# Four small moves in the order of an attention and feed-forward kernel on one core

## The chip, the core and the metric

The kernel runs on one core of a Trainium2 chip. A core has five engines that work side by side, each through its own queue of instructions, in order: TensorE (PE, matrix products and transposes; its weight loads are listed as PEld), VectorE (DVE), ScalarE (ACT), GpSimd (POOL) and SyncE (SP, which here only issues transfers). PE writes its results to PSUM, eight banks of 128 x 512 fp32 words; the others read PSUM or SBUF. Engines wait for each other through semaphores. The metric is the time of one execution in microseconds. The three runs of the kernel before took 175.51, 175.60 and 176.47 us; the median is 175.6.

## The reference

Windowed attention with a few global keys, and then a feed-forward part with the largest of three products. Batch 4, 8 heads, 768 positions, head dimension 64; 8 global keys, a window of 96; model width 512, inner width 768.

```python
scores = scale * np.matmul(q, k.transpose(0, 1, 3, 2))
is_global = pos[None, :] < n_global
is_local = (rel >= 0) & (rel < n_local)          # rel = row position - column position
dist = np.where(is_global & ~is_local, n_local, np.abs(rel))
scores = np.where(is_global | is_local, scores - slopes * dist, -1e9)
a = softmax(scores)                              # 1e-9 added to the sum
x = (a @ v), heads joined                        # 3072 x 512
h = np.maximum(np.maximum(x @ w1, x @ w2), x @ w3)
out = h @ w_out                                  # 3072 x 512, float32
```

## The kernel before

The 3072 rows are 24 tiles T of 128 rows, six to a batch. Two tiles (256 positions) form a group G, in which q and k are loaded, cast to bf16 and transposed together. Because the window is 96, tile T needs only its own keys, those of tile T - 1, and the 8 global keys, which are copied into rows of tile T - 1 that the window can't reach. The feed-forward part works on chunks of 4, 2, 2, 4, 4, 4 and 4 tiles (`SIZES`).

Nothing schedules this program. Its order is a string, `SCHEDULE`, of 782 units, written out in the source; the loop at the end of the kernel calls one small function for each. The place of a unit in the string sets its place in the queue of its engine and nothing else: units of different engines drift apart as far as the semaphores let them. A unit reads as a letter, its arguments, often with the engine last (0 ACT, 1 DVE, 2 POOL, 3 a DMA), and after `@` the buffer or bank that it takes. Those that the text needs:

- `l a.G.p` (SP, lines 229 and 236): load q (a = 0), k (1) or v (2) of group G, 512 KB in 512-byte pieces. `l0.7.2` is q of group 7, tiles 14 and 15.
- `c a.G.p.how` (lines 195 and 201): cast q or k of the group to bf16. On ACT or DVE it is one instruction of 128x1024, on POOL two of 128x512. `v T.e.how` (254) casts half of a tile's v.
- `X T` (SP, 292): transpose a tile's q and k by a DMA, from SBUF to SBUF. `G` (313, 315) and `V` (321 to 325) copy global keys and values.
- `S T.g` (PE, 349): scores of four heads; `e` (ACT, 356): their exponentials; `m` (DVE, 365 and 367): times the bias and window mask; `A T` (PE, 391 and 394): times v; `n T` (DVE, 402 and 403): divide by the sum, into `xb`.
- `Z T` (SP, 424): transpose the attention output of a tile by a DMA, from `xb` to `xT`; for a few tiles `t` and `u` do that on PE and ACT (418, 421).
- `F c.f.j` (PE, 433): 128 inner columns f of product j for chunk c, four matmuls. `f` (447, 449, 452) empties the bank: j = 0 a cast, j = 1 a maximum, j = 2 a maximum into `ht`.
- `O c.t` (PE, 457): one output tile, six matmuls; `o` (471) copies it to SBUF; `s` (SP, 477) stores it, in one transfer, or in two halves where the last argument is 2. `E` (PE, 457; 462, 463): the four output tiles of the last chunk, copied and stored as they come, the last of them in pieces of 256, 128 and 128 columns, the first two stored by SP and the third by ACT's own queue.

A bank or buffer that a unit takes has to be free: `F3.1.2@4` and then `A13@4` take bank 4, so A13 waits until `f3.1.2.1` has read it. A wait of the first instruction in a queue holds everything behind it.

Around the changed places the string reads, before (units of all engines):

```
Z8@0 V10.1.0 l0.7.2@2 v11.1.2 ... n10 ... Z9 ... m12.1.1 e13.0@2 c0.7.2.1@1 Z10 f2.0.1.1 m13.1.1
v13.0.1 l1.9.2@0 c1.9.2.1 F3.0.2@0 F3.0.1@5 f3.0.1.1 F3.1.2@4 f3.0.2.1@1 ... l1.7.2@6 c1.7.2.2 f3.1.2.1
V16.1.2 f4.3.0.0@0 v20.0.2 G18.0 ... c0.11.2.2@1 ... V16.0.2 ... c0.10.2.2@2 A19@2 ... G19.0 s0.1 V19.0.2
f6.5.2.1 E@7 O5.0@2 o5.0.0@5 s5.0.2
```

Of the kernel before, what the change touches and what calls it, by code (L numbers as in the profile page):

```python
# [21 lines left out]


SCHEDULE = """
    l0.12.1@0 l1.12.1@1 D10.512@0 l1.12.3@2 l0.12.2@3 l0.12.3@4 R K7 K6 B1.1 K4 B2.1 K2 B3.0 K1 K5 B0.1 B6.1
# [28 lines left out]
    v15.1.2 v12.1.2 F2.5.2@0 O1.1@1 v12.0.2 S12.1.0@2 e12.1@3 S13.1.0@4 m11.0.1 Z9 f2.5.2.1 S13.0.0@6
    o1.1.1@5 F2.4.2@0 A11@2 n11@2 F2.0.1@1 e13.1@1 F2.3.1@4 m12.0.1 m12.1.1 e13.0@2 c0.7.2.1@1 Z10 f2.0.1.1
    m13.1.1 F2.0.2@5 f2.3.1.1 t11@2 F2.1.2@3 l0.9.2@3 l1.8.2@4 u11.0 G13.0 f2.1.2.1 f2.0.2.1 F2.3.2@6
    F3.4.0@2 F3.0.0@1 f3.4.0.0@4 f3.0.0.1@0 m13.0.1 v13.1.1 f2.4.2.1 F3.1.0@4 F3.3.0@5 c0.9.2.0@2 f3.3.0.0@1
    A12@2 n12@1 f2.3.2.1 f3.1.0.1@2 F3.1.1@1 f3.1.1.1 v13.0.1 l1.9.2@0 c1.9.2.1 F3.0.2@0 F3.0.1@5 f3.0.1.1
    F3.1.2@4 f3.0.2.1@1 F3.2.0@1 F3.2.2@2 l1.7.2@6 c1.7.2.2 f3.1.2.1 F3.5.0@3 A13@4 V13.1.1 f3.5.0.1@3 n13@0
    l2.9.2@2 l0.8.2@5 c0.8.2.2@0 v19.0.2 V13.0.0 f3.2.0.0@0 v14.0.2 F3.5.1@0 l2.8.2@1 F3.2.1@6 f3.2.1.1  # L60
    f3.2.2.1 F3.3.1@1 F3.5.2@3 v18.1.0 X14@3 v14.1.2 X15 f3.5.1.1 f3.3.1.1 F3.4.1@2 c1.8.2.0 S14.0.0@4
    S14.1.0@0 e14.0@6 G14.2 f3.4.1.1 F3.4.2@6 f3.5.2.1 F3.3.2@7 e14.1@7 f3.4.2.1 m14.0.1 m14.1.1 v19.1.2
    v15.0.2 S15.0.0@0 e15.0@0 S15.1.0@2 G15.1 e15.1@5 f3.3.2.1 O2.0@6 A14@0 V14.1.2 o2.0.1@6 n14@3 X18@0
    O2.1@7 v18.0.0 o2.1.0@7 m15.0.1 S18.0.0@0 S18.1.0@2 X19 Z13@1 V14.0.1 O3.3@6 m15.1.1 e18.0@3 e18.1@4
    X16@1 o3.3.0@8 A15@0 n15@2 O3.0@7 S19.1.0@0 v17.1.1 m18.0.1 S16.1.0@2 m18.1.1 e19.1@1 S16.0.0@4 O3.2@6
    o3.0.1@9 e16.0@2 V15.1.2 A18@0 e16.1@6 n18@0 o3.2.1@10 m16.1.1 X17 O3.1@7 G16.0 Z14 o3.1.0@11 m16.0.1
    V15.0.1 S17.0.0@0 v16.0.0 Z12 S19.0.0@2 Z15 e19.0@7 S17.1.0@4 e17.1@0 m17.1.1 F4.4.0@6 e17.0@5 l0.11.2@1
    s1.0 l2.10.2@0 F4.2.0@7 l1.10.2@2 F4.1.0@2 F4.5.0@3 v16.1.0 F4.3.0@0 A16@4 f4.2.0.0@2 Z18@2 V16.1.2
    f4.3.0.0@0 v20.0.2 G18.0 F4.1.2@1 f4.1.0.1@3 c0.11.2.2@1 m17.0.1 v17.0.1 l2.11.2@2 n16@3 s3.1 f4.5.0.0@4
    V16.0.2 m19.0.1 l0.10.2@3 F4.0.1@0 F4.1.1@7 m19.1.1 f4.4.0.0@1 F4.5.2@6 c0.10.2.2@2 A19@2 Z16 n19@1 Z19  # L70
    G19.0 s0.1 V19.0.2 s2.1 f4.1.1.1 f4.1.2.1@0 V19.1.1 F4.0.0@4 F4.4.1@5 A17@2 c1.10.2.0 f4.0.0.1@3 n17@2
    F4.5.1@7 f4.5.1.1 F4.2.1@1 F4.3.2@4 f4.5.2.1 f4.4.1.1 F4.0.2@2 F4.3.1@3 F4.4.2@5 f4.2.1.1 v22.1.1
    f4.0.1.1 f4.3.1.1 f4.0.2.1 f4.3.2.1 F4.2.2@1 Z17 F5.1.1@0 F5.2.0@3 F5.5.0@2 s1.1 F5.3.0@4 F5.0.0@6
    f4.2.2.1 f5.3.0.0@4 f5.0.0.0@3 v21.1.2 F5.1.0@1 s0.0 l1.11.2@0 F5.3.1@4 c1.11.2.2 f5.2.0.1@0 f4.4.2.1
    v23.0.2 F5.0.1@3 v21.0.2 f5.1.0.1@2 f5.1.1.1 s2.0 X20@2 S20.0.0@0 v22.0.1 S20.1.0@6 f5.0.1.1 G20.2
    f5.5.0.0@1 e20.0@3 e20.1@4 F5.5.1@2 f5.5.1.1 F5.2.2@3 v20.1.2 f5.3.1.1 F5.2.1@5 m20.1.1 F5.4.0@2
    f5.2.1.1 m20.0.1 f5.2.2.1@1 F5.1.2@4 f5.1.2.1 X21 f5.4.0.0@0 s3.3 X23@3 s0.3 S21.1.0@0 S21.0.0@6 e21.0@2
    F5.0.2@3 X22 f5.0.2.1 v23.1.2 e21.1@6 s0.2 A20@4 F5.4.1@2 V20.0.1 m21.0.1 F5.4.2@3 G21.1 S22.1.0@0
# [533 lines left out]
```

## Time and profile before

| | |
|---|---|
| median of three runs | 175.6 us |
| span of the profiled execution, first to last instruction | 174.8 us |
| mean granted clock of PE | 0.996 |
| PE busy | 165.9 us, 95% |
| DVE busy | 131.9 us, 75% |
| ACT busy | 95.4 us, 55% |
| POOL busy | 54.7 us, 31% |
| read from and written to HBM | 25.17 and 6.29 MB |

The page gives the profiled execution's span alone; the time of that execution as the runs measure it is not on the page, and the median of the runs lies 0.8 us above the span. "L433" is line 433 of the kernel. A row of a timeline gives the start in us, the busy time, the engine, the line, the operation, what it writes and reads, how many instructions were merged, and in brackets how long the engine had been idle and what ended that. Row ends can overlap the next start by some 0.08 us on DVE and ACT, and on PE by more, since its instructions are pipelined and their ends are modelled. A transfer has two times: SP's row is the time that issuing took, and the landing is listed separately, counted from the issue.

### The profile page before, as it was taken

Reading aid. Unit: us, or ns where it says so; the run is one execution under the profiler, and the core shown is the slowest. Engines: PE = TensorE matmul, PEld = TensorE weight load, DVE = VectorE, ACT = ScalarE, POOL = GpSimd, SP = SyncE. Lnnn points to the kernel's source line nnn. Section 1 sums busy time; section 2 is a strip of 40 time slices with the busy share of each in tenths; the row PEclk is TensorE's granted clock in tenths of the full one; section 3 lists DMA queues with packets and bytes.
Section 4 is the critical chain, followed back from the end, with each engine's and each line's share of the span. In section 5 each row is a group of like instructions: output and inputs, shape, how many; then the busy total and the mean of one; then the engine's idle time right before and its main releaser. Section 6 shows DMA issues by size and latency. Waiting matters only on the chain.

```text
span 174.8 us, 3865 instructions
## 1 busy us (share of the span) xinstructions
PE 165.9 (95%) x1485; PEld 93.6 (54%) x1507; DVE 131.9 (75%) x268; ACT 95.4 (55%) x147; POOL 54.7 (31%) x99
## 2 busy tenths in 40 slices
PE   7997999999999999898999999999999999999991
PEld 2555745577676877544445545544445554444460
DVE  7889864988599897989898678899578993074910
ACT  5988897672868788440667688200345651402051
...
GB/s 149 352 292 327 402 360 385 270 371 311 229 303 179 139 183 266 267 290 284 165 135 112 114 145 306 305 210 260 231 213 20 0 120 137 121 286 4 0 119 185
DMA packets 66403, 37.36 MB, mean 214 GB/s; under 512 B 24144, under 2 KB 61392, under 8 KB 66384
## 3 DMA queue, kind: packets, MB, share of 16 engines
...
q10 hardware_dynamic: 144, 0.07, 0.1%
q14 instruction: 7, 0.06, 0.1%
HBM read 25.17 MB, written 6.29 MB: 180 GB/s over the span
## 4 chain that ended last, share of the span: by engine, by line
PE 76%; DVE 10%; DMA 6%; ACT 3%; issue 2%; SPq 0%; DVEq 0%
PE psum L433 44%; PE psum L457 17%; PE psum L349 6%; DMA xT<-xb 3%; DMA rawqk<-in_k_dram 3%; DVE P L365 3%; PE psum L391 3%; PE psum L394 2%; PE psum L276 2%; DVE ht L452 1%; DVE xb L403 1%; ACT P L356 1%; PE psum L270 1%; DVE qb L195 1%; PE psum L335 1%
## 5 line engine op out<-in xcount | busy, mean ns | idle before, releaser
L433 PE MATMUL psum<-xT,w 128*128 128x512 bf16 (+1 forms) x491 | 97.5, 348 | 1.5 <-DMA xT<-xb 0.7
L433 PEld LDWEIGHTS <-w 128*128 128x128 bf16 x504 | 47.6, 98 | 42.9 <-DMA xT<-xb 0.9
L356 ACT ACTIVATE P<-psum 128x1024 bf16<-128x1024 f32 (+1 forms) x48 | 43.3, 954 | 10.4 <-PE psum L349 10.3
L449 DVE TENSOR_TENSOR h<-h,psum 128x512 bf16<-128x512 bf16 (+1 forms) x42 | 25.0, 605 | 15.9 <-PE psum L433 12.4
L457 PE MATMUL psum<-wo,ht 128*128 128x512 bf16 (+2 forms) x147 | 33.4, 362 | 0.5
L447 ACT CAST h<-psum 128x512 bf16<-128x512 f32 (+1 forms) x27 | 13.8, 523 | 33.1 <-PE psum L433 29.8
L452 DVE TENSOR_TENSOR ht<-h,psum 128x512 bf16<-128x512 bf16 (+1 forms) x42 | 26.2, 644 | 2.1 <-PE psum L433 0.9
L365 DVE TENSOR_TENSOR P<-P,wmask 128x1024 bf16<-128x1024 bf16 x34 | 25.2, 752 | 2.0 <-ACT P L356 1.7
L457 PEld LDWEIGHTS <-ht 128*128 128x128 bf16 x156 | 13.8, 98 | 13.5 <-DVE ht L452 0.2
L254 POOL CAST va<-rawv 64x512 bf16<-64x512 f32 x28 | 18.5, 668 | 4.8 <-DMA rawv<-in_v_dram 3.7
L323 POOL COPY va<-vaf 4x260 int32<-4x260 int32 x17 | 7.2, 424 | 34.9 <-PE psum L394 34.5
L403 DVE TENSOR_TENSOR xb<-psum,rz 128x512 bf16<-128x512 f32 x24 | 16.6, 692 | 0.8
L201 POOL CAST qb<-rawk 128x512 bf16<-128x512 f32 x12 | 7.5, 654 | 23.7 <-DMA rawk<-in_k_dram 23.7
L349 PE MATMUL psum<-qkT 64*128 64x128 bf16 x352 | 14.4, 217 | 0.5 <-DVE qkT L315 0.4
L391 PEld LDWEIGHTS <-P 128*128 128x128 bf16 x192 | 12.6, 97 | 3.2 <-ACT P L356 0.4
L349 PEld LDWEIGHTS <-qkT 64*128 64x128 bf16 x352 | 10.0, 94 | 7.9 <-issue 5.9
L391 PE MATMUL psum<-va,P 128*128 128x65 bf16 x160 | 12.7, 193 | 0.7 <-DVE ht L452 0.6
L447 DVE CAST h<-psum 128x512 bf16<-128x512 f32 (+1 forms) x15 | 9.1, 615 | 5.1 <-PE psum L433 5.1
L471 ACT COPY staging<-psum 128x512 f32<-128x512 f32 x14 | 8.2, 592 | 8.8 <-PE psum L457 8.8
L201 POOL CAST qb<-rawq 128x512 bf16<-128x512 f32 x14 | 8.9, 664 | 9.0 <-DMA rawq<-in_q_dram 5.0
L394 PEld LDWEIGHTS <-P 128*128 128x128 bf16 x160 | 10.5, 97 | 2.1 <-issue 0.7
L394 PE MATMUL psum<-va,P 128*128 128x65 bf16 x128 | 9.9, 193 | 0.0
...
## 6 DMA issues: line engine op xcount, KB each, us to landing
...
out_dram<-staging SPq DMA_DIRECT2D x5, 128.0 KB, 2.2
```

Of the source, the lines that this page charges most:

```text
L254: copies[how](heads(va(T))[64 * e:64 * e + 64, :, 0:D], src)
L349: nc.tensor.matmul(sp[:, hh, j2, ds], qT(T - ds, 1, hsl, jp), qT(T, 0, hsl, jp), start=not how, stop=True, skip_group_check=True)
L356: nc.scalar.activation(P[:, :, 0:n], sps[T, g].rearrange("p a b d n -> p (a b) d n")[:, :, 0:n], AF.Exp, bias=0.0, scale=scale)
L365: mul(P, P, wmask[:, g, :, 0:2])
L391: nc.tensor.matmul(o, P[:, i, 0], heads(va(T))[:, h], start=True, stop=(t == 0), skip_group_check=True)
L394: nc.tensor.matmul(o, P[:, i, 1], heads(va(T - 1))[:, h], start=False, stop=True, skip_group_check=True)
L403: nc.vector.tensor_tensor(out=x.rearrange("p (g h) d -> p g h d", g=2), in0=o4[:, :, :, 0:64], in1=rz[:, :, :, None].to_broadcast([128, 2, ...
L433: nc.tensor.matmul(ps, w123[f // 2][:, j, dm, (f % 2) * 128:(f % 2) * 128 + 128], xT[c][:, dm], start=(dm == 0), stop=(dm == 3))
L447: copies[how](h01, ps)
L449: nc.vector.tensor_max(h01s[c, f], h01s[c, f], ps)
L452: nc.vector.tensor_max(dst, h01s[c, f].rearrange("p (t e i) -> p t e i", e=2, i=64), ps.rearrange("p (t e i) -> p t e i", e=2, i=64))
L457: nc.tensor.matmul(po, ht[c][:, f, tt * 128:(tt + 1) * 128], wo[:, f, cols], start=(f == 0), stop=(f == NF - 1))
```

## The change

All four moves are in the string; no function changes, and the numbers of all units but three stay as they are.

1. `l0.7.2`, the load of q for group 7, is issued after the transposes `Z9` and `Z10` instead of before them. Its cast `c0.7.2.1` on DVE moves from after `m12.1.1` to after `v13.1.1`.
2. The casts of k for groups 9 and 7 swap engines: `c1.9` goes from DVE to POOL, `c1.7` from POOL to DVE, there behind `f3.0.1.1`. The load `l1.7.2` is written earlier, with the same neighbours in SP's queue.
3. POOL's order around tile 19: before `V16.1, v20.0, c0.11, V16.0, c0.10, V19.0`; after `V16.1, V16.0, V19.0, v20.0, c0.11, c0.10`.
4. `O5.0`, its copy and its store come before `E` instead of after it, and the store is one transfer instead of two halves. The last piece of the program is then E's 128-column part.

In the diff most lines differ only because the string is wrapped anew; cut to the units that move:

```diff
-    ... Z8@0 V10.1.0 l0.7.2@2 v11.1.2 v15.1.2
+    ... Z8@0 V10.1.0 v11.1.2 v15.1.2
...
-    ... m12.0.1 m12.1.1 e13.0@2 c0.7.2.1@1 Z10 f2.0.1.1
+    ... m12.0.1 m12.1.1 e13.0@2 Z10 l0.7.2@2 f2.0.1.1
...
-    f3.4.0.0@4 f3.0.0.1@0 m13.0.1 v13.1.1 f2.4.2.1
+    f3.4.0.0@4 f3.0.0.1@0 m13.0.1 v13.1.1 c0.7.2.1@1 f2.4.2.1
...
-    ... v13.0.1 l1.9.2@0 c1.9.2.1 F3.0.2@0 F3.0.1@5 f3.0.1.1
-    F3.1.2@4 f3.0.2.1@1 F3.2.0@1 F3.2.2@2 l1.7.2@6 c1.7.2.2 f3.1.2.1
+    ... v13.0.1 l1.9.2@0 l1.7.2@6 c1.9.2.2 F3.0.2@0 F3.0.1@5 f3.0.1.1
+    c1.7.2.1 F3.1.2@4 f3.0.2.1@1 F3.2.0@1 F3.2.2@2 f3.1.2.1
...
-    ... V16.1.2 f4.3.0.0@0 v20.0.2 G18.0 F4.1.2@1 f4.1.0.1@3 c0.11.2.2@1 m17.0.1
-    ... s3.1 f4.5.0.0@4 V16.0.2 m19.0.1 ... F4.5.2@6 c0.10.2.2@2 A19@2 Z16 n19@1 Z19 G19.0 s0.1 V19.0.2 s2.1
+    ... V16.1.2 V16.0.2 f4.3.0.0@0 G18.0 F4.1.2@1 f4.1.0.1@3 m17.0.1
+    ... s3.1 f4.5.0.0@4 m19.0.1 ... F4.5.2@6 A19@2 V19.0.2 v20.0.2 c0.11.2.2@1 c0.10.2.2@2 Z16 n19@1 Z19 G19.0 s0.1 s2.1
...
-    F6.5.0@1 f6.5.0.1@2 F6.5.2@5 f6.5.1.1 f6.5.2.1 E@7 O5.0@2 o5.0.0@5 s5.0.2
+    F6.5.0@1 f6.5.0.1@2 F6.5.2@5 f6.5.1.1 f6.5.2.1 O5.0@2 o5.0.0@5 s5.0 E@7
```

More of the change, by code (lines that the diff above doesn't have):

```diff
@@ L54 @@
[L54 to L78, printed above, removed]
@@ L84 @@
-    f6.4.0.1@0 F6.1.1@4 f6.4.1.1 f6.4.2.1 s4.3 s4.0 f6.3.0.0@4 F6.3.2@1 F6.1.0@2 s5.2 F6.2.1@3 s4.2 s5.1
-    s4.1 f6.1.0.0@1 s3.0 s5.3.2 f6.3.1.1 f6.1.1.1 f6.3.2.1 f6.2.1.1 F6.2.2@2 f6.2.2.1 f6.1.2.1 F6.5.1@4
-    F6.5.0@1 f6.5.0.1@2 F6.5.2@5 f6.5.1.1 f6.5.2.1 E@7 O5.0@2 o5.0.0@5 s5.0.2
+    y1.0.1.1@1 y1.1.1.0 x12.0.2@0 e1.1@0 c1.12.2.1 x12.0.3 y0.0.0.1 l1.2.2@0 y1.0.0.1 x12.1.3@1 x12.1.2 y0.1.0.0
+    S0.1.1 e0.1@1 G0.1 b2.1@6 v2.0.2 v3.0.2 w1.0@0 S1.0.1 G1.0 e1.0@2 b2.0@2 w0.0@0 y1.1.0.1 S2.1.1 w1.1@1
@@ new lines @@
+    X12@2 G10.1 G12.1 F2.4.1@7 A9@4 V9.1.2 V9.0.2 X13 O1.0@6 l2.7.2@0 n9@0 S12.0.0@0 f2.4.1.1 m10.0.1 l2.6.2@1
+    v10.1.1 e12.0@4 S11.1.0@2 S11.0.0@4 e11.1@5 F2.2.2@7 f2.2.2.1@0 F2.3.0@0 F2.1.1@1 F2.0.0@7 f2.3.0.0@3
+    m10.1.1 e11.0@0 f2.0.0.0@1 A10@2 V10.0.2 f2.1.1.1 m11.1.1 o1.0.0@4 n10@3 Z8@0 V10.1.0 v11.1.2 v15.1.2
+    v12.1.2 F2.5.2@0 O1.1@1 v12.0.2 S12.1.0@2 e12.1@3 S13.1.0@4 m11.0.1 Z9 f2.5.2.1 S13.0.0@6 o1.1.1@5 F2.4.2@0
+    A11@2 n11@2 F2.0.1@1 e13.1@1 F2.3.1@4 m12.0.1 m12.1.1 e13.0@2 Z10 l0.7.2@2 f2.0.1.1 m13.1.1 F2.0.2@5
@@ new lines @@
+    f2.3.1.1 t11@2 F2.1.2@3 l0.9.2@3 l1.8.2@4 u11.0 G13.0 f2.1.2.1 f2.0.2.1 F2.3.2@6 F3.4.0@2 F3.0.0@1
+    f3.4.0.0@4 f3.0.0.1@0 m13.0.1 v13.1.1 c0.7.2.1@1 f2.4.2.1 F3.1.0@4 F3.3.0@5 c0.9.2.0@2 f3.3.0.0@1 A12@2
+    n12@1 f2.3.2.1 f3.1.0.1@2 F3.1.1@1 f3.1.1.1 v13.0.1 l1.9.2@0 l1.7.2@6 c1.9.2.2 F3.0.2@0 F3.0.1@5 f3.0.1.1
+    c1.7.2.1 F3.1.2@4 f3.0.2.1@1 F3.2.0@1 F3.2.2@2 f3.1.2.1 F3.5.0@3 A13@4 V13.1.1 f3.5.0.1@3 n13@0 l2.9.2@2
+    l0.8.2@5 c0.8.2.2@0 v19.0.2 V13.0.0 f3.2.0.0@0 v14.0.2 F3.5.1@0 l2.8.2@1 F3.2.1@6 f3.2.1.1 f3.2.2.1 F3.3.1@1
@@ new lines @@
+    F3.5.2@3 v18.1.0 X14@3 v14.1.2 X15 f3.5.1.1 f3.3.1.1 F3.4.1@2 c1.8.2.0 S14.0.0@4 S14.1.0@0 e14.0@6 G14.2
+    f3.4.1.1 F3.4.2@6 f3.5.2.1 F3.3.2@7 e14.1@7 f3.4.2.1 m14.0.1 m14.1.1 v19.1.2 v15.0.2 S15.0.0@0 e15.0@0
+    S15.1.0@2 G15.1 e15.1@5 f3.3.2.1 O2.0@6 A14@0 V14.1.2 o2.0.1@6 n14@3 X18@0 O2.1@7 v18.0.0 o2.1.0@7 m15.0.1
+    S18.0.0@0 S18.1.0@2 X19 Z13@1 V14.0.1 O3.3@6 m15.1.1 e18.0@3 e18.1@4 X16@1 o3.3.0@8 A15@0 n15@2 O3.0@7
+    S19.1.0@0 v17.1.1 m18.0.1 S16.1.0@2 m18.1.1 e19.1@1 S16.0.0@4 O3.2@6 o3.0.1@9 e16.0@2 V15.1.2 A18@0 e16.1@6
@@ new lines @@
+    n18@0 o3.2.1@10 m16.1.1 X17 O3.1@7 G16.0 Z14 o3.1.0@11 m16.0.1 V15.0.1 S17.0.0@0 v16.0.0 Z12 S19.0.0@2 Z15
+    e19.0@7 S17.1.0@4 e17.1@0 m17.1.1 F4.4.0@6 e17.0@5 l0.11.2@1 s1.0 l2.10.2@0 F4.2.0@7 l1.10.2@2 F4.1.0@2
+    F4.5.0@3 v16.1.0 F4.3.0@0 A16@4 f4.2.0.0@2 Z18@2 V16.1.2 V16.0.2 f4.3.0.0@0 G18.0 F4.1.2@1 f4.1.0.1@3
+    m17.0.1 v17.0.1 l2.11.2@2 n16@3 s3.1 f4.5.0.0@4 m19.0.1 l0.10.2@3 F4.0.1@0 F4.1.1@7 m19.1.1 f4.4.0.0@1
+    F4.5.2@6 A19@2 V19.0.2 v20.0.2 c0.11.2.2@1 c0.10.2.2@2 Z16 n19@1 Z19 G19.0 s0.1 s2.1 f4.1.1.1 f4.1.2.1@0
@@ new lines @@
+    V19.1.1 F4.0.0@4 F4.4.1@5 A17@2 c1.10.2.0 f4.0.0.1@3 n17@2 F4.5.1@7 f4.5.1.1 F4.2.1@1 F4.3.2@4 f4.5.2.1
+    f4.4.1.1 F4.0.2@2 F4.3.1@3 F4.4.2@5 f4.2.1.1 v22.1.1 f4.0.1.1 f4.3.1.1 f4.0.2.1 f4.3.2.1 F4.2.2@1 Z17
+    F5.1.1@0 F5.2.0@3 F5.5.0@2 s1.1 F5.3.0@4 F5.0.0@6 f4.2.2.1 f5.3.0.0@4 f5.0.0.0@3 v21.1.2 F5.1.0@1 s0.0
+    l1.11.2@0 F5.3.1@4 c1.11.2.2 f5.2.0.1@0 f4.4.2.1 v23.0.2 F5.0.1@3 v21.0.2 f5.1.0.1@2 f5.1.1.1 s2.0 X20@2
+    S20.0.0@0 v22.0.1 S20.1.0@6 f5.0.1.1 G20.2 f5.5.0.0@1 e20.0@3 e20.1@4 F5.5.1@2 f5.5.1.1 F5.2.2@3 v20.1.2
@@ new lines @@
+    f5.3.1.1 F5.2.1@5 m20.1.1 F5.4.0@2 f5.2.1.1 m20.0.1 f5.2.2.1@1 F5.1.2@4 f5.1.2.1 X21 f5.4.0.0@0 s3.3 X23@3
+    s0.3 S21.1.0@0 S21.0.0@6 e21.0@2 F5.0.2@3 X22 f5.0.2.1 v23.1.2 e21.1@6 s0.2 A20@4 F5.4.1@2 V20.0.1 m21.0.1
+    F5.4.2@3 G21.1 S22.1.0@0 S22.0.0@6 G22.0 e22.1@1 f5.4.1.1 e22.0@7 m21.1.1 f5.4.2.1 V20.1.1 n20@0 O4.0@2
+    m22.1.1 F5.3.2@3 f5.3.2.1 A21@0 n21@3 m22.0.1 S23.1.0@4 e23.1@0 S23.0.0@6 e23.0@5 O4.1@3 F5.5.2@0 m23.1.1
+    Z21@0 V21.1.1 m23.0.1 V21.0.2 A22@4 V22.0.2 V22.1.1 n22@1 s3.2 Z20 o4.1.0@4 O4.3@1 A23@6 O4.2@3 Z22
@@ new lines @@
+    o4.3.0@11 f5.5.2.1 O5.2@0 O5.3@1 n23@2 O5.1@4 o5.3.0@1 Z23 F6.4.2@1 o4.0.1@7 F6.0.0@2 F6.0.2@5 F6.0.1@6
+    o5.2.0@5 F6.1.2@0 o5.1.0@3 F6.4.0@4 F6.2.0@7 f6.0.0.0@2 f6.0.1.1 F6.4.1@2 f6.0.2.1@0 F6.3.1@5 o4.2.0@6
+    f6.2.0.1@3 F6.3.0@3 f6.4.0.1@0 F6.1.1@4 f6.4.1.1 f6.4.2.1 s4.3 s4.0 f6.3.0.0@4 F6.3.2@1 F6.1.0@2 s5.2
+    F6.2.1@3 s4.2 s5.1 s4.1 f6.1.0.0@1 s3.0 s5.3.2 f6.3.1.1 f6.1.1.1 f6.3.2.1 f6.2.1.1 F6.2.2@2 f6.2.2.1
+    f6.1.2.1 F6.5.1@4 F6.5.0@1 f6.5.0.1@2 F6.5.2@5 f6.5.1.1 f6.5.2.1 O5.0@2 o5.0.0@5 s5.0 E@7
```

54 lines of the change are left out of this document (22 added, 32 removed).

## The prediction

> **What bounds the kernel.** I read the page first, then a table of stretches, then the chain of waits, then the timelines of single engines around the places the change touches.
>
> ```profile
> span 174.8 us, 3865 instructions
> PE 165.9 (95%) x1485; PEld 93.6 (54%) x1507; DVE 131.9 (75%) x268; ACT 95.4 (55%) x147; POOL 54.7 (31%) x99
> L433 PE MATMUL psum<-xT,w 128*128 128x512 bf16 (+1 forms) x491 | 97.5, 348 | 1.5 <-DMA xT<-xb 0.7
> ```
>
> TensorE is busy 95% of the span, so no other engine's time counts by itself. A move can only pay where PE stands still, and the stretches say where that is (columns: stretch, length, then busy time of each engine, granted clock, DMA share, GB/s).
>
> ```profile
> 73.00:84.00 11.00, 10.36 (x68) 5.15 (x69) 9.23 (x18) 2.40 (x4) 2.15 (x3) 1.00 1.18 286
> 102.00:112.00 10.00, 9.78 (x84) 5.07 (x80) 7.68 (x13) 7.52 (x13) 2.92 (x5) 1.00 1.06 277
> 112.00:165.00 53.00, 52.68 (x361) 25.70 (x366) 38.57 (x69) 14.98 (x22) 6.68 (x13) 1.00 0.56 142
> 171.20:174.80 3.60, 0.00 (x0) 0.00 (x0) 0.00 (x0) 0.58 (x1) 0.00 (x0) 0.81 0.43 143
> ```
>
> From 112 to 165 us PE idles 0.32 us in 53, that is 0.06 per 10 us: this is what "full" looks like. Between 73 and 84 it idles 0.64, between 102 and 112 it idles 0.22, and after 171.2 nothing runs but one copy and its store. The timeline of PE shows the holes themselves.
>
> ```profile
> 71.12 1.04 PE L433 MATMUL psum<-xT,w 128*128 128x256 bf16 x8
> 72.81 3.63 PE L433 MATMUL psum<-xT,w 128*128 128x512 bf16 x15 [0.66 <-DMA xT<-xb]
> ...
> 83.12 0.19 PE L391 MATMUL psum<-va,P 128*128 128x65 bf16 x1 [0.59 <-DVE ht L452]
> ...
> 88.14 0.62 PE L349 MATMUL psum<-qkT 64*128 64x128 bf16 x16
> ```
>
> Two holes: 0.66 us at 72.81, where F3.4.0 waits for the transposed tile 10 (Z10), and 0.59 at 83.12, where A13 waits for f3.1.2.1 on DVE to empty its bank. The third figure to keep is 88.14, where S14 starts.
>
> **Move 1, l0.7 behind Z9 and Z10.** First SP's queue, with the landing times of three single transfers (us from issue: Z10's; a transpose with nothing ahead of it, issued at 139.99; X14's), and the line of an instruction fetch, which the view of transfers gives for 70.4 to 71.6 us and again for 86.9 to 88.3; then DVE; then ACT and POOL.
>
> ```profile
> 64.79 0.58 SPq L236 DMA_DIRECT2D rawq<-in_q_dram  x1
> 65.45 3.55 SPq L424 DMA_TRANSPOSE xT<-xb  x2
> 69.05 0.57 SPq L236 DMA_DIRECT2D rawq<-in_q_dram  x1
> 69.68 4.53 SPq L236 DMA_DIRECT2D rawk<-in_k_dram  x3
> ...
> 81.60 1.54 SPq L292 DMA_TRANSPOSE qkT<-qb  x1
> ```
> ```profile
> xT<-xb SPq DMA_TRANSPOSE x1, 5.0
> ...
> xT<-xb SPq DMA_TRANSPOSE x1, 2.4
> ...
> qkT<-qb SPq DMA_TRANSPOSE x1, 4.9
> ...
> q8 instruction: 1, 0.02, 5.6%
> ```
> ```profile
> 66.69 0.69 DVE L403 TENSOR_TENSOR xb<-psum,rz 128x512 bf16<-128x512 f32 x1
> ...
> 71.38 0.69 DVE L195 CAST qb<-rawq 128x1024 bf16<-128x1024 f32 x1
> ...
> 74.75 0.69 DVE L447 CAST h<-psum 128x512 bf16<-128x512 f32 x1 [0.74 <-PE psum L433]
> 75.36 0.68 DVE L365 TENSOR_TENSOR P<-P,wmask 128x1024 bf16<-128x1024 bf16 x1
> ...
> 79.51 0.43 DVE L254 CAST va<-rawv 64x512 bf16<-64x512 f32 x1
> 79.97 1.13 DVE L195 CAST qb<-rawk 128x1024 bf16<-128x1024 f32 x1
> ...
> 81.73 1.33 DVE L452 TENSOR_TENSOR ht<-h,psum 128x512 bf16<-128x512 bf16 x2
> ```
> ```profile
> 71.32 0.59 ACT L421 COPY xT<-psum 128x512 bf16<-128x512 bf16 x1 [0.57 <-PE psum L418]
> ...
> 79.94 1.63 POOL L201 CAST qb<-rawk 128x512 bf16<-128x512 f32 x2 [10.13 <-DMA rawk<-in_k_dram]
> ```
>
> Z9 now issues where l0.7 did, at 64.79. Z10 cannot issue before n10 ends (66.69 + 0.69 = 67.38), so it goes at about 67.45 instead of 67.78, with 512 KB less ahead of it. It lands between 67.45 + 2.4 = 69.9 and 67.45 + 5.0 = 72.45; I take about 70, since the load is gone. F3.4.0 then waits for nothing: the matmuls before it end at 71.12 + 1.04 = 72.16, and tile 11's copy on ACT at 71.32 + 0.59 = 71.91. So the hole of 0.66 at 72.81 goes.
>
> But what is late next is DVE. From 74.75 to 83.06 it runs almost without a pause, and A13 waits for its end. The chain starts at F3.0.0's eviction at 74.75, which now comes earlier: by 0.66, or by up to 0.8 if F3.4.0 can start at 72.0, since the 256-column matmuls before it are pipelined and their modelled ends lie late. Move 1 also carries c0.7 (0.69 us at 71.38) to behind v13.1.1, so from a place where DVE afterwards idled 0.74 into the chain itself. The chain's rest therefore starts between 0.03 later and 0.1 earlier; I take 0.1 earlier. Nearly all of the hole at 72.81 goes into that cast and comes back before A13.
>
> The price is on the loads. l0.7 used to run while Z9 and Z10 waited; now it is issued at about 67.45 + 1.2 = 68.7, near l0.9's old 69.05, and l0.9, l1.8, l1.9, l1.7, l2.9, l0.8 and l2.8 queue behind it. At 286 GB/s a 512 KB load takes 1.8 us. If the rings find other work all the while, the later loads lose nothing; if they stand empty for that whole time, 1.8. I take 0.7, nearer the lower end, because Z9, Z10 and the fetch fill part of it. POOL's wait shows l1.7 landing at 79.94, so it lands at about 80.6.
>
> **Move 2, c1.9 to POOL and c1.7 to DVE** (with l1.7's unit written earlier; its place in SP's order does not change). Before, the two casts ran at once: DVE's took 1.13 us, where the same 128x1024 cast alone took 0.69 (71.38). Now POOL takes c1.9 on its landing, some two microseconds ahead, and DVE does c1.7 after f3.0.1.1, with POOL idle: 1.13 - 0.69 = 0.44 off the chain. DVE reaches c1.7 at 79.51 - 0.1 + 0.43 + 0.7 = 80.54, about when l1.7 lands; I put that wait at 0.1. So f3.1.2.1 ends at 83.06 - 0.1 - 0.44 + 0.1 = 82.6 and A13 starts 0.45 earlier. Bounds: without the wait 0.55 gained; with l1.7 at 79.94 + 1.8 = 81.74 it ends at 81.74 + 0.69 + 1.33 = 83.76, 0.7 lost. POOL's queue behind c1.9 (c0.8, v19, v14) waits for l0.8 anyway. X14 needs c1.7: its end moves from 81.57 (POOL) to about 81.3.
>
> Where POOL's c1.9 meets v13.0.1 there may be a second price. See move 3's rows.
>
> **Move 3, POOL around tile 19.** DVE, POOL and SP there:
>
> ```profile
> 108.19 2.86 DVE L365 TENSOR_TENSOR P<-P,wmask 128x1024 bf16<-128x1024 bf16 x2
> ...
> 108.54 1.16 POOL L201 CAST qb<-rawq 128x512 bf16<-128x512 f32 x2
> ...
> 119.57 4.07 SPq L292 DMA_TRANSPOSE qkT<-qb  x2
> ```
>
> The two mask products of tile 19 took 2.86 us; one takes 0.68 (75.36), so the pair lost about 1.5 beside POOL's v20, c0.11 and V16.0. PE felt little of it: 0.22 - 0.06 = 0.16 idle between 102 and 112. Afterwards POOL does V16.0, then V19.0, which waits for A19, and only then the casts. m19 runs free, and PE gains between 0 and 0.16; I take 0.1. The casts now lie beside n19 and maxima that read PSUM. V16.0 comes earlier for A17; v20, c0.11 and c0.10 are first read by S20's side of the queue, whose transposes SP issues from 119.57 on, so a few microseconds of lateness cost nothing.
>
> The Trainium skill ("SBUF — State Buffer", section "Who interferes with whom") says that a DVE instruction with two SBUF inputs, or a copy or cast in a 2-port mode, is blocked for the whole length of a GpSimd instruction that holds the shared pair. This case's 2.86 us agree with it. By it, v13.0.1 would lose a half of POOL's c1.9 in move 2 if they meet; without it, nothing.
>
> **Move 4, E last.** O5.0 moves ahead of E; matmuls, copies and bytes are the same, so PE still ends at about 171.19.
>
> ```profile
> 167.67 3.15 SPq L463 DMA_DIRECT2D out_dram<-staging  x5
> ...
> 169.90 0.27 ACT L462 COPY staging<-psum 128x128 f32<-128x128 f32 x1 [0.30 <-PE psum L457]
> 170.19 0.37 ACTq L463 DMA_DIRECT2D out_dram<-staging  x1
> 171.19 0.58 ACT L471 COPY staging<-psum 128x512 f32<-128x512 f32 x1 [1.03 <-PE psum L457]
> 171.80 0.81 SPq L477 DMA_DIRECT2D out_dram<-staging  x2
> ```
> ```profile
> out_dram<-staging ACTq DMA_DIRECT2D x1, 64.0 KB, 2.1
> ...
> out_dram<-staging SPq DMA_DIRECT2D x2, 128.0 KB, 1.7
> ```
>
> Before, the end is a 0.58 copy and two issues: the second starts at about 172.2 and lands 1.7 to 1.8 later, at 174.0. Afterwards E's pieces come one O5.0 later (169.90 to 171.19 is 1.29): the last copy is 0.27, ACT issues at 170.19 + 1.29 = 171.48, SP's fifth store at about 170.41 + 1.29 = 171.7. With 2.1 to land, as those 64 KB stores took behind E's others, the end is at 173.8, 0.2 better. With the 1.7 of the stores that met no queue it is at 173.4, 0.6 better, and 0.8 if SP's five issues also run shorter than their 3.15. I take 0.4. O5.0 needs bank 2, which DVE empties before the last F6 matmuls; E's wait for ht 5 gets 1.29 us more cover.
>
> **Sum.** 0.45 + 0.1 + 0.4 = 0.95 us. The profiled span of 174.8 becomes 173.85. The median of the runs, 175.6, stands 0.8 above the span; the same gain on it gives 174.65, and I forecast 174.6.
>
> **Rivals.**
> (a) More is gained: l1.7 lands as before, A13 gains 0.55, A19 0.16, the tail 0.8: 1.5, so 174.1. For it: the tail before had two issues on one queue.
> (b) l1.7 lands 1.8 late, DVE holds its queue for it, and A13 loses up to 0.7: 0.7 - 0.1 - 0.4 = +0.2, 175.8. At 1.2 late it loses 0.1 and the sum is 175.2. For it: DMA share is 1.18 from 73 to 84, so nothing makes up for a gap. Against: the fetch and Z10's own packets overlap the gap.
> (c) POOL's c1.9 blocks v13.0.1 for one of its halves, 1.16 / 2 = 0.58: the 0.45 becomes -0.15, so 175.25. It needs l1.9 to land near 79, not 78.
> (d) Slower: X14 comes too late. It lands at 81.60 + 4.9 = 86.5, 1.64 before S14's 88.14. With the loads 1.8 late it lands at 88.3, and with an instruction fetch in its way (5.6% of 16 engines over 1.2 us is 1.1 us on one of them) at 89.4. PE then waits 1.26 at S14, less 0.1 and 0.3: 176.5. It decides from a landing after 88.14. Against: before, that later fetch came at 86.9, after X14 had landed, and X14 itself is issued no later than before.
> (e) Move 1 does not do what it says: Z10 was late through the fetch, not the load, and still lands near 72.8. Then c0.7 is 0.69 more in a chain that starts as before: 0.69 - 0.44 = +0.25 at A13, less 0.5: 175.35.
>
> **How the numbers follow.** A difference of 0.5% is 0.88 us, about what runs of this kernel can tell from none. Forecast 0.45 (own range 174.2 to 175.0; the bound lies at 174.72, so I put 0.28 of the 0.45 beyond it), (a) 0.2, (b) 0.1, (c) 0.08, (d) 0.1, (e) 0.07. Faster: 0.28 + 0.2 = 0.48; slower: (d) and 0.03 of (b) with more queueing, 0.13; same: the rest, 0.39. The range reaches from just under (a) to (b), 173.9 to 175.8, and leaves (d) and the tails outside.
>
> **What would show it.** Right: no PE idle for xT near 72; one hole before A13, shorter than the 0.66 and 0.59 together and ended by DVE; c1.7 on DVE at about 0.69; the m19 pair near 1.3; ACT's 128x128 copy last and the last store a 64 KB one. Wrong: DVE idle for rawk near 80 (b), v13.0.1 well over 0.43 (c), PE idle for qkT before S14 (d), Z10 still 5 us in flight (e).

## The result, and the profile after

The kernel after takes 176.88 us (median of 22 executions, 175.70 to 177.75), the kernel before beside it 175.88 us (22 executions, 175.36 to 177.00). The ratio is 1.0054, 95% interval 1.0038 to 1.0070: slower by about 0.95 us. The ratios, here and below, are not exactly the quotients of the two medians; gains and losses in us go by the ratios. The forecast was 174.6 with a range of 173.9 to 175.8, so both its sign and its range were wrong.

The profiled execution of after has a span of 175.0 us and a time of 176.8. Where a span and a time of one execution are both listed, the time stands about 1.8 above the span. By that, the profile of before, span 174.8, was of an execution of some 176.6 us, about 0.7 above the median of its kernel. This returns below. Line numbers of the code in after are two lower than in before: L431 is before's L433.

First the page of after (span and busy times), then the table of stretches, with the columns of the one before.

```profile
span 175.0 us, 3887 instructions
PE 167.2 (96%) x1507; PEld 93.6 (53%) x1507; DVE 130.6 (75%) x268; ACT 95.3 (54%) x147; POOL 53.6 (31%) x99
```
```profile
73.00:84.00 11.00, 10.08 (x68) 4.81 (x66) 8.88 (x18) 2.21 (x4) 1.33 (x2) 1.00 1.16 292
102.00:112.00 10.00, 9.13 (x83) 4.74 (x78) 6.01 (x12) 7.68 (x13) 0.79 (x2) 1.00 0.99 249
112.00:165.00 53.00, 53.00 (x376) 25.77 (x373) 38.15 (x68) 14.98 (x22) 8.41 (x16) 1.00 0.57 149
172.00:175.00 3.00, 0.00 (x0) 0.00 (x0) 0.00 (x0) 0.25 (x1) 0.00 (x0) 1.00 0.50 175
```

PE idles 0.92 from 73 to 84 where it idled 0.64, and 0.87 from 102 to 112 where it idled 0.22. From 112 on it is full, and the stretch with PE done is 3.0 instead of 3.6. The 0.32 that before idled from 112 to 165 is no waiting: its page counts 1485 matmuls where after's counts 1507, and the missing records leave six gaps of 0.05. A second profile of before that has all 1507 is full there too. The timeline of PE in after shows the holes:

```profile
71.32 2.98 PE L431 MATMUL psum<-xT,w 128*128 128x256 bf16 x17
...
83.22 0.19 PE L389 MATMUL psum<-va,P 128*128 128x65 bf16 x1 [0.89 <-DVE ht L450]
...
103.42 4.48 PE L431 MATMUL psum<-xT,w 128*128 128x512 bf16 x20 [0.87 <-DVE P L363]
```

The hole at F3.4.0 near 72 is gone. The one before A13 has grown from 0.59 to 0.89. A third, of 0.87, stands at 103.42, at F4.4.0, a place that the prediction does not name. Set against the profile of before, A13 starts 0.10 later (83.22 against 83.12), F4.4.0 1.09 later (103.42 against 102.33), and the span ends 0.2 later: 0.6 of it comes back in the tail and 0.3 at A19. There PE in before (timeline of PE) stood between the first four heads and the last four, until the second mask product of tile 19 ended at 108.19 + 2.86 = 111.05:

```profile
110.80 0.19 PE L394 MATMUL psum<-vaf,P 128*128 128x65 bf16 x1
111.11 0.20 PE L391 MATMUL psum<-va,P 128*128 128x65 bf16 x1
```

The starts of these small matmuls lie 0.03 apart otherwise, and in after here too. From F4.4.0's start to PE's last end PE takes 68.5 us in after and in the second profile of before, so what F4.4.0 loses is not made up.

The chain of waits of after goes through the changed place:

```profile
68.85 0.57 SPq L234
...
74.04 7.17 DMA rawk<-in_k_dram
81.23 0.69 DVE qb L193
81.92 1.25 DVE ht L450 x2
...
83.22 0.19 PE psum L389
```

Read from the top: l0.7 is issued at 68.85, behind Z10, and four more loads behind it until l1.7 at 74.04. l1.7 lands 7.17 later, at 81.21; c1.7 and f3.1.2.1 run on DVE, and A13 starts. A load now sets A13's start. In before DVE's own work did.

For the third hole the chain names a mask product on DVE (L363). That is the wait that came last by the profile, at 103.31. In before the same two products (timeline of DVE) still ran when F4.4.0 started (timeline of PE):

```profile
101.88 1.28 DVE L365 TENSOR_TENSOR P<-P,wmask 128x1024 bf16<-128x1024 bf16 x2
```
```profile
102.33 0.61 PE L433 MATMUL psum<-xT,w 128*128 128x512 bf16 x2
```

They ended at 103.16 and F4.4.0 started at 102.33, so F4.4.0 does not wait for them. It reads `xT` of the tiles that Z12 to Z15 write, and Z15 lands at 103.33 in after (issued at 100.83, 2.5 to landing), 0.09 before F4.4.0's start.

### The profile page after: what moved, and what is told of

Read it like the earlier page. It is cut to its first block, busy times and chain, and to the rows that moved or that the text cites. A ratio compares the mean times of both kernels' runs of the same rounds, so it can differ in the third digit from the quotient of the medians.

```text
span 175.0 us, 3887 instructions
## 1 busy us (share of the span) xinstructions
PE 167.2 (96%) x1507; PEld 93.6 (53%) x1507; DVE 130.6 (75%) x268; ACT 95.3 (54%) x147; POOL 53.6 (31%) x99
## 4 chain that ended last, share of the span: by engine, by line
PE 76%; DVE 8%; DMA 7%; SPq 3%; ACT 2%; issue 2%; DVEq 0%
PE psum L431 46%; PE psum L455 17%; PE psum L347 5%; DMA rawk<-in_k_dram 4%; SPq L234 3%; DMA rawqk<-in_k_dram 3%; PE psum L389 2%; PE psum L392 2%; DVE P L363 2%; PE psum L274 1%; ACT P L354 1%; DVE ht L450 1%; PE psum L268 1%; PE psum L333 1%; DVE xb L401 1%
## 5 line engine op out<-in xcount | busy, mean ns | idle before, releaser
L431 PE MATMUL psum<-xT,w 128*128 128x512 bf16 (+1 forms) x504 | 98.8, 349 | 1.0 <-DVE P L363 0.9
L431 PEld LDWEIGHTS <-w 128*128 128x128 bf16 x504 | 47.6, 98 | 43.1 <-issue 1.5
L455 PE MATMUL psum<-wo,ht 128*128 128x512 bf16 (+2 forms) x156 | 33.9, 363 | 0.2 <-DVE h L447 0.2
L363 DVE TENSOR_TENSOR P<-P,wmask 128x1024 bf16<-128x1024 bf16 x34 | 24.2, 723 | 2.3 <-ACT P L354 2.2
L252 POOL CAST va<-rawv 64x512 bf16<-64x512 f32 x28 | 19.1, 689 | 3.8 <-DMA rawv<-in_v_dram 2.7
```

Source lines behind the costliest of these rows:

```text
L252: copies[how](heads(va(T))[64 * e:64 * e + 64, :, 0:D], src)
L363: mul(P, P, wmask[:, g, :, 0:2])
L431: nc.tensor.matmul(ps, w123[f // 2][:, j, dm, (f % 2) * 128:(f % 2) * 128 + 128], xT[c][:, dm], start=(dm == 0), stop=(dm == 3))
L455: nc.tensor.matmul(po, ht[c][:, f, tt * 128:(tt + 1) * 128], wo[:, f, cols], start=(f == 0), stop=(f == NF - 1))
```

## The experiments

### Each move alone

Four kernels, each the kernel before with one move. Move 1 (load and cast):

```diff
-    ... Z8@0 V10.1.0 l0.7.2@2 v11.1.2 ... e13.0@2 c0.7.2.1@1 Z10 f2.0.1.1 ... v13.1.1 f2.4.2.1
+    ... Z8@0 V10.1.0 v11.1.2 ... e13.0@2 Z10 l0.7.2@2 f2.0.1.1 ... v13.1.1 c0.7.2.1@1 f2.4.2.1
```

> Move 1 alone (l0.7 behind Z9 and Z10, c0.7 behind v13.1.1). Theory A, late loads: the 512 KB load that used to run while Z10 waited for n10 now starts after Z10, all later loads land about 1.4 us later (POOL's wait for l1.7 ends near 81.3 instead of 79.9), X14 and the transposes behind it on SP follow, Z15 lands near 103.3 and F4.4.0 waits for it about 1 us: slower by 0.8 to 1.3 us. Rival B, the swap of casts is what costs: move 1 alone is within 0.3 us of before, or faster by up to 0.5. Rival C, the new order at the end or of POOL costs: within 0.3 us.

Move 2 (the casts of k swapped):

```diff
-    ... l1.9.2@0 c1.9.2.1 F3.0.2@0 F3.0.1@5 f3.0.1.1 F3.1.2@4 ... l1.7.2@6 c1.7.2.2 f3.1.2.1
+    ... l1.9.2@0 l1.7.2@6 c1.9.2.2 F3.0.2@0 F3.0.1@5 f3.0.1.1 c1.7.2.1 F3.1.2@4 ... f3.1.2.1
```

> Move 2 alone (c1.9 to POOL, c1.7 to DVE, loads as before). Theory A: l1.7 lands near 79.9, DVE does not wait for it, the cast takes 0.69 instead of 1.13 us, A13 starts 0.3 to 0.5 earlier and nothing later takes it back: faster by 0.1 to 0.5 us. Rival B: DVE's queue is held by c1.7 and A13 starts later: slower by 0.5 to 1 us. Rival C: within 0.3 us.

Move 3 (POOL's order around tile 19):

```diff
-    V16.1.2 f4.3.0.0@0 v20.0.2 G18.0 ... c0.11.2.2@1 ... V16.0.2 ... c0.10.2.2@2 A19@2 ... V19.0.2
+    V16.1.2 V16.0.2 f4.3.0.0@0 G18.0 ... A19@2 V19.0.2 v20.0.2 c0.11.2.2@1 c0.10.2.2@2 ...
```

> Move 3 alone (POOL's order around tile 19). Theory A and rival B: the two mask products of tile 19 take 1.3 to 1.4 us instead of 2.9, PE gains 0.1 to 0.2 at A19: faster by 0 to 0.2 us. Rival C: the later casts c0.11 and c0.10 hold X20 or X22 and it is slower by 0.3 us or more.

Move 4 (E last):

```diff
-    f6.5.2.1 E@7 O5.0@2 o5.0.0@5 s5.0.2
+    f6.5.2.1 O5.0@2 o5.0.0@5 s5.0 E@7
```

> Move 4 alone (O5.0 before E, one store). Theory A and rival B: the time from PE's end to the end of the span falls from 3.6 to about 3.0 us: faster by 0.2 to 0.6 us. Rival C: PE waits at O5.0 for bank 2 or the stores crowd at the end: slower by 0.3 us or more.

Measured beside the kernel before on one chip (175.99 us):

| kernel | us | ratio, 95% interval |
|---|---|---|
| move 1 alone | 177.21 | 1.0078 [1.0054, 1.0103] |
| move 2 alone | 175.83 | 0.9986 [0.9971, 1.0000] |
| move 3 alone | 175.98 | 1.0000 [0.9981, 1.0019] |
| move 4 alone | 175.26 | 0.9959 [0.9939, 0.9979] |

The whole loss is move 1's. The four add up to +0.23% (0.78 - 0.14 + 0 - 0.41); the intervals of the four, added as squares, give that sum roughly 0.4 either way (roughly, because the four share the runs of before), which holds the 0.54 that was measured. Move 1's loss, 1.4 us, is a little more than the 0.8 to 1.3 expected, and move 4's gain, 0.7, a little more than its 0.2 to 0.6.

The holes of move 1 alone lie elsewhere than in after (timeline of PE):

```profile
82.55 0.19 PE L391 MATMUL psum<-va,P 128*128 128x65 bf16 x1 [0.34 <-DVE ht L452]
...
88.81 0.62 PE L349 MATMUL psum<-qkT 64*128 64x128 bf16 x16 [1.25 <-DMA qkT<-qb]
```

PE reached S14 at 87.56 and waited 1.25 for X14, which landed at 88.76; F4.4.0, where the wait was expected, then had no hole. So the lateness is paid at S14 in one execution and at F4.4.0 in another. The profile of move 3 alone shows a hole for Z10 at F3.4.0 (0.44, at 73.19); those of move 2 and move 4 alone show none, with Z10 landing at 71.80 and 72.09.

### The load put back, and the load halfway

Next, after with `l0.7.2` alone back in its old place, the late cast `c0.7` kept; and after with the load between Z9 and Z10 in SP's queue.

```diff
-    ... Z8@0 V10.1.0 v11.1.2 ... e13.0@2 Z10 l0.7.2@2 f2.0.1.1
+    ... Z8@0 V10.1.0 l0.7.2@2 v11.1.2 ... e13.0@2 Z10 f2.0.1.1
```

> The changed kernel with one thing undone: l0.7 is issued ahead of Z9 and Z10 again; its cast c0.7 stays behind v13.1.1, and moves 2, 3 and 4 stay. Theory A (the place of the load costs, through l0.8, l1.7, l2.8 and X14 to S14 or F4.4.0): the loads land as before, l1.7 near 79.5 to 79.9, no wait of PE at S14 or F4.4.0, faster than before by 0.5 to 1.1 us. Rival D (the cast c0.7 in DVE's chain costs): still slower than before by 0.5 us or more.

```diff
-    ... Z10 l0.7.2@2 f2.0.1.1
+    ... l0.7.2@2 Z10 f2.0.1.1
```

> The changed kernel with l0.7 between Z9 and Z10 instead of behind both. Theory A: the load is issued near 66.5, while Z10 would wait for n10 anyway until 67.4, so the rings have work and the later loads land within 0.3 us of before: faster than before by 0.5 to 1.1 us, like the kernel with the load put back. If instead any delay of the load matters in proportion (one of two transposes ahead of it): about half the loss, within 0.4 us of before.

Against 175.75 of before on the same chip, the kernel with the load put back takes 175.43, ratio 0.9976 [0.9960, 0.9992], and the one with the load halfway 175.80, ratio 1.0003 [0.9983, 1.0022]. Putting back the one load turns +0.54% into -0.24%: 0.78%, or 1.4 us, by one transfer's place in a queue. The gain on before, 0.4 us, is a little less than expected, but the kernel is not slower than before, so rival D, the late cast, is out. The holes of the kernel with the load put back (timeline of PE; no hole at S14, and none at F4.4.0):

```profile
82.50 0.19 PE L391 MATMUL psum<-va,P 128*128 128x65 bf16 x1 [0.20 <-DVE ht L452]
```
```profile
101.73 2.55 PE L433 MATMUL psum<-xT,w 128*128 128x512 bf16 x11
```

Every transfer behind the load is late by about as much. Landing times (issue plus time to landing, for the last of the sixteen engines):

| transfer | after | load halfway | load put back | before |
|---|---|---|---|---|
| Z10 | 71.75 | 71.88 | 72.09 | 72.77 |
| l0.7 | 73.31 | 69.75 | 69.56 | 70.19 |
| l1.7 | 81.21 | 80.31 | 79.15 | 79.82 |
| l2.8 | 86.44 | 85.51 | 84.37 | 84.84 |
| X14 | 88.20 | 87.18 | 85.48 | 86.50 |
| Z15 | 103.33 | 102.04 | 101.33 | 101.80 |

Between after and the kernel with the load put back the lateness is 2.06 at l1.7, 2.07 at l2.8, 2.72 at X14 and still 2.00 at Z15, 22 us further on. Little there could make it up: in after the DMA share is 1.20 from 75 to 85, and SP issues the ten transposes from 82.07 to 102.04 with one pause of 0.6. The profile with the load put back is the one with the earliest l1.7. In the nine profiles with the load ahead of Z9 it lands between 79.15 and 80.23, with a median of 79.54; in the three with the load behind Z10 and Z12 in its place it lands between 81.17 and 81.34, some 1.7 later. For Z15 the same groups without Z12's move are 100.88 to 101.87 and once 102.17, against 103.05 to 103.33. The table of stretches says where it arose; first two rows of after, then two of the kernel with the load put back.

```profile
0.00:74.00 74.00, 71.06 (x780) 46.04 (x781) 60.67 (x140) 55.77 (x87) 37.86 (x69) 1.00 1.01 273
0.00:80.00 80.00, 77.03 (x813) 48.75 (x814) 66.32 (x152) 57.30 (x89) 38.26 (x70) 1.00 1.03 275
```
```profile
0.00:74.00 74.00, 70.55 (x780) 45.77 (x781) 59.96 (x140) 55.98 (x88) 38.45 (x69) 1.00 1.05 282
0.00:80.00 80.00, 76.52 (x814) 48.48 (x815) 65.63 (x152) 57.49 (x89) 39.61 (x71) 1.00 1.06 283
```

The last column is GB/s. By 80 us after had moved 275 x 80 us = 22.0 MB and the other 22.6: 0.6 MB less, about the one load of 0.52 MB. All fourteen profiles agree: counted from the packets, by 71 us the ten with the load ahead of Z10 had moved 19.99 to 20.05 MB, the four with it behind 19.52 to 19.55. In after Z8 and Z9 have landed by 68.91, and until l0.7's packets follow Z10 is nearly alone: the DMA share of the single microseconds from 68 to 71 is 0.53, 0.55 and 0.37. With the load put back it is 1.20, 1.16 and 0.38.

The kernel halfway came out about halfway, but I can't say that this is the same emptiness by half: its l0.9 landed at 73.81, as with the load put back (73.73), and it lost its 1.1 us between l0.9 and l1.8 (2.88 instead of 1.81), a step that before also shows in another execution (2.52). By 71 us it had moved 20.02 MB, as much as with the load put back. The expectation that it would equal the put-back kernel was missed.

### Moves 2, 3 and 4 without move 1, and before once more

The kernel of moves 2, 3 and 4 is before with those three diffs. The fourth kernel of this set is before itself, to see what its holes do in another execution.

> Moves 2, 3 and 4 together, move 1 left out whole. Theory A: the single results add, -0.25, 0 and -0.7 us: faster than before by 0.7 to 1.2 us. If the moves need each other: within 0.5 us.

> The kernel before, looked at once more. If the hole of 0.66 us at F3.4.0 in the first profile belongs to every execution, Z10 lands near 72.8 and PE waits 0.5 us or more there; if it belonged to that execution, as the profiles of moves 2 and 4 alone suggest (Z10 at 71.8 and 72.1, no hole), Z10 lands near 72 and PE waits less than 0.3 us. Time within 0.3% of before.

Moves 2 to 4 take 175.23, ratio 0.9961 [0.9941, 0.9980], 0.7 us faster, the least that was expected of a sum. PE has no hole from 64 to 112, and the span is 173.2. This beats both kernels; move 4 alone (0.9959, another chip) is no different by these intervals. The kernel with the load put back differs from it only in the late cast `c0.7`: 0.9976 against 0.9961, so that half of move 1 is worth about 0.15%, less than either interval's width.

Before once more: 176.02, ratio 1.0005 [0.9986, 1.0025], span of the profiled execution 174.5. It has no hole at F3.4.0 (Z10 landed at 71.99), but one at F4.4.0:

```profile
102.25 4.48 PE L433 MATMUL psum<-xT,w 128*128 128x512 bf16 x20 [0.59 <-issue]
```

Z15 landed at 102.17 there, 0.08 before. So the row of transposes already bounded F4.4.0 in some executions of before, and the 0.66 at F3.4.0 that move 1 was to remove belongs to some executions, not to the kernel: of the nine profiles with the load ahead of Z9, two have a hole there (0.66 in the first, 0.44 in move 3's).

The waits that moves 2 and 3 were to remove are no more constant. In this execution the cast of k for group 9 took 0.69 on DVE beside POOL's cast, where the first profile had 1.13, and the two mask products of tile 19 took 1.69, where it had 2.86 (timelines of DVE and POOL):

```profile
79.77 0.69 DVE L195 CAST qb<-rawk 128x1024 bf16<-128x1024 f32 x1
...
108.11 1.69 DVE L365 TENSOR_TENSOR P<-P,wmask 128x1024 bf16<-128x1024 bf16 x2
```
```profile
79.97 1.51 POOL L201 CAST qb<-rawk 128x512 bf16<-128x512 f32 x2 [9.53 <-DMA rawk<-in_k_dram]
...
108.14 1.12 POOL L254 CAST va<-rawv 64x512 bf16<-64x512 f32 x1 [0.43 <-DMA rawv<-in_v_dram]
109.21 1.62 POOL L201 CAST qb<-rawq 128x512 bf16<-128x512 f32 x2
```

Here POOL's casts were the slower ones (1.51, 1.12 and 1.62; alone 1.16, 0.61 and 1.16), and there is no hole at A13 or A19. Five profiles have these two casts of k side by side as before has them, and in four of them DVE's took 0.69 or 0.70. Six have POOL's old order at tile 19: the pair took 2.86 and 2.88 in two (before, and move 2 alone), 1.69 to 1.87 in four, and PE waited at A19 in the two alone.

### One transpose taken out of the row

If the row of transposes carries the loss, a transpose moved ahead should give it back. Z12, whose tile is ready early, goes among the loads, ahead of l2.8; once on after, once on before, once on moves 2 to 4.

```diff
-    ... l0.8.2@5 c0.8.2.2@0 ... Z13@1 ... Z12 S19.0.0@2 Z15
+    ... l0.8.2@5 Z12@1 c0.8.2.2@0 ... Z13 ... S19.0.0@2 Z15
```

> The changed kernel, and Z12 (its input is ready since n12, near 77.7) issued behind l0.8, where SP waits for v13.0.1 anyway, instead of between Z14 and Z15. Theory A, second half (the late loads reach PE only through the row of transposes from X14 to Z15, for which F4.4.0 waits): the row is one transpose shorter, Z15 is issued 1 to 1.5 us earlier, the hole of 0.87 us at F4.4.0 goes, A13 stays where it was: 0.6 to 1.1 us faster than the changed kernel, so within 0.4 us of before. Rival E (F4.4.0 waits for the mask product m16.0.1 or another engine, as the profile's chain names it): no change, 0.9 us slower than before.

> The kernel before, with Z12 moved the same way and nothing else. If Z15 bounds F4.4.0 in it too (0.59 us hole in its second profile, none in the first): faster by 0.2 to 0.6 us. If not: within 0.2 us. If Z12's 128 KB ahead of l2.8 make X14 late: slower.

> Moves 2, 3 and 4, and Z12 early. With Z15 off the edge A13's gain is kept in every execution: 0.2 to 0.5 us faster than moves 2, 3 and 4, 0.9 to 1.4 faster than before. If F4.4.0 does not wait there: like moves 2, 3 and 4, 0.7 faster than before.

Beside 175.96 of before: on after 177.58, ratio 1.0112 [1.0074, 1.0150]; on before 176.18, 1.0017 [0.9999, 1.0036]; on moves 2 to 4 175.49, 0.9978 [0.9961, 0.9994]. In none did it help, and on after it cost. The timeline of PE on after:

```profile
84.14 0.19 PE L391 MATMUL psum<-va,P 128*128 128x65 bf16 x1 [1.17 <-DVE ht L452]
...
90.59 0.62 PE L349 MATMUL psum<-qkT 64*128 64x128 bf16 x16 [1.45 <-DMA qkT<-qb]
```

The hole at F4.4.0 did go, as the theory says, but the lateness came out earlier: l2.8 landed at 88.15 and X14 at 90.55, 1.7 and 2.35 later than in after, and PE waited 1.45 at S14. Not all of it is the edit's: l1.7, which stands ahead of Z12, landed at 82.13, already 0.9 late in this execution, and PE had lost 0.66 more at 78.70, ahead of Z12's place. With Z12 in it the step from l0.8 to l2.8 took 2.81 instead of 1.63. The other two kernels, whose l1.7 was not late, show a hole at S14 too, of 0.52 and 0.42, with X14 landing at about 87.5. There it was X14's last part that came late: its first part landed at 85.68 in both, as in before (85.72), the last 1.85 behind it, beside an instruction fetch that ran from 85.3 to 86.6 (in before it came at 87.0, after X14). Whether the edit moved the fetch is not tested. The expectation of a gain was missed: no hole stands at F4.4.0 in any of the three, and S14 waits in each.

### After once more

> The changed kernel, looked at once more. Theory A: in this execution too l1.7 lands 1 us or more later than in the kernel with the load put back (79.2) and PE has a hole of 0.5 us or more at S14 (behind X14) or at F4.4.0 (ending within 0.15 us of Z15's landing); 0.8 to 1.2 us slower than before. Rival E (F4.4.0 waits for m16.0.1 on DVE): the hole ends with that product and not with Z15's landing.

176.65 us, ratio 1.0042 [1.0022, 1.0062], span 175.0: 0.7 us slower than before, somewhat less than expected. In this execution the loss is paid at all three places (timeline of PE):

```profile
83.36 0.19 PE L389 MATMUL psum<-va,P 128*128 128x65 bf16 x1 [1.33 <-DVE ht L450]
...
88.78 0.62 PE L347 MATMUL psum<-qkT 64*128 64x128 bf16 x16 [0.42 <-DMA qkT<-qb]
...
103.27 4.48 PE L431 MATMUL psum<-xT,w 128*128 128x512 bf16 x19 [0.24 <-issue]
```

l1.7 landed at 81.34 and Z15 at 103.18, within 0.15 of the first profile. No hole at S14 or F4.4.0 reaches the 0.5 that was expected. Rival E is out: the two mask products ran from 102.51 to 103.79, and F4.4.0 started before they ended. The loads' lateness belongs to the kernel; how it is divided among A13, S14 and F4.4.0 varies, and F4.4.0's start comes out nearly the same (103.27 and 103.42).

## Why the prediction was wrong

**Move 1, the hole at F3.4.0: it went, but had not been the kernel's.** "The hole of 0.66 at 72.81 goes" came true, but by less than the step that the prediction gave. Z10 was to land at about 70. Its first part landed at 69.89, its last at 71.75: 1.0 earlier than in the profile of before, not 2.8, and only 0.05 to 0.45 earlier than in the kernels of moves 2, 4, 2 to 4 and before once more (71.80 to 72.20), where the load stands ahead of it. Rival (e) was half right: most of Z10's lateness was not the load's, though Z10 did not stay near 72.8. The 0.66 hole came from a profile whose execution was about 0.7 longer than the median; seven of the eight other profiles with the load ahead don't have it.

**Move 1, the price: the step that failed, twice.** First its size. "I take 0.7, nearer the lower end" for the later loads; they came 1.39 later than in the profile of before and 2.06 later than with the load alone put back, some 1.7 later by the medians of all profiles: nearly the upper bound of 1.8. The reason given, that Z9, Z10 and the fetch fill part of the gap, did not hold: Z9 had landed at 68.91, and Z10 and the fetch kept the DMA share near 0.5 where the loads make it 1.2. DVE's timeline in after shows rival (b)'s sign, and that the rest of the prediction's DVE chain was near:

```profile
79.48 0.42 DVE L252 CAST va<-rawv 64x512 bf16<-64x512 f32 x1
79.94 0.69 DVE L447 TENSOR_TENSOR h<-h,psum 128x512 bf16<-128x512 bf16 x1
81.23 0.69 DVE L193 CAST qb<-rawk 128x1024 bf16<-128x1024 f32 x1 [0.60 <-DMA rawk<-in_k_dram]
81.84 1.32 DVE L450 TENSOR_TENSOR ht<-h,psum 128x512 bf16<-128x512 bf16 x2
```

DVE reached c1.7 at 80.63 (predicted 80.54), the cast took 0.69 (predicted), and then it waited 0.60 for l1.7 (predicted 0.1). A13 came 0.10 later instead of 0.45 earlier.

Second, what lay behind A13. With l1.7 at the 81.21 that was measured, the prediction's own sum would have been +0.2 at A13, -0.1 for move 3 and -0.4 for move 4: still 0.3 faster. The rest of the loss is at F4.4.0, 1.09 later than in before, and the prediction never followed the late loads that far. It checked one consumer, S14, and found 1.64 of slack. Z15, the last of the ten transposes behind the loads, landed at 101.80 in before, and F4.4.0 started at 102.33: 0.53 of slack. In after Z15 was 1.53 later, 1.0 more than that; PE, itself 0.1 late, waited 0.87.

**Rival (d)** had the right kind of place, X14 and S14, and an argument against it that failed: "X14 itself is issued no later than before". It was issued at 82.07, not 81.60, and took 6.1 us instead of 4.9, because l2.8, ahead of it, landed 1.60 later (86.44 against 84.84): of the 1.70 that X14 was late, 1.60 were there without any instruction fetch. X14 landed at 88.20. In the profile of after S14 escapes by 0.05; in move 1 alone and in after once more it does not (1.25 and 0.42). That the 1.25 is so near the rival's 1.26 is luck: X14 landed at 88.76 there, not at 89.4, and PE was at S14 early, at 87.56.

**Move 2**: the cast took the 0.69 that was said of it, but the 1.13 it was priced against was the one execution's; in four others with the old order it took 0.69 or 0.70 already, so the 0.44 was mostly not there to win. Alone the move measures 0.14% (interval 0 to 0.29%), 0.25 us, which is not clear of nothing; in after DVE waits for l1.7. Rival (c) did not happen in after: v13.0.1 took 0.42 from 79.48, with POOL's c1.9 beside it from 79.60:

```profile
79.60 1.33 POOL L199 CAST qb<-rawk 128x512 bf16<-128x512 f32 x2 [9.59 <-DMA rawk<-in_k_dram]
```

**Move 3**: the mask products of tile 19 came down to 0.68 each, from a pair of 2.86. The row groups the three from 106.8 to 109.9 us, tile 19's last:

```profile
L363 DVE TENSOR_TENSOR P<-P,wmask x3: 681/683/684, 106.8 to 109.9; 128x1024 bf16<-128x1024 bf16 x3
```

The time did not change (1.0000, within 0.19%), which holds the 0.1 us that was taken. The working behind that 0.1 misread the profile: the 0.06 per 10 us that it took for a full PE were missing records, and in that execution the wait at A19 was 0.3. In four of six executions with the old order PE did not wait there, which fits a move that gains nothing in most.

**Move 4**: 0.41% or 0.7 us alone, near the upper end of the 0.2 to 0.8 given; 0.4 was taken. In after the tail shows the stores in the order foreseen (timeline of ACT, its queue and SP's):

```profile
169.76 2.81 SPq L461 DMA_DIRECT2D out_dram<-staging  x5
...
171.98 0.27 ACT L460 COPY staging<-psum 128x128 f32<-128x128 f32 x1 [0.30 <-PE psum L455]
172.28 0.37 ACTq L461 DMA_DIRECT2D out_dram<-staging  x1
```
```profile
out_dram<-staging ACTq DMA_DIRECT2D x1, 64.0 KB, 1.8
```

The last store takes 1.8 to land, nearer the 1.7 of a store that meets no queue than the 2.1 that gave the low end, and SP's issues run 2.81 instead of 3.15.

**What stays open.** It is not shown whether an instruction fetch is what makes the last part of Z10 land 1.7 to 2.1 us behind the first in all kernels but the halfway one. The fourteen traces point to it: 49 of their 406 transposes on SP have a last part more than 0.8 us behind the first, and beside every one of these (at most 0.9 us ahead of its first landing, or later) a 16 KB packet of the fetch queue runs; of the other 357 transposes 27 have one. No kernel was made without the fetch. It is not known either what decides in an execution whether S14 or F4.4.0 pays.
